# Storing the output of four batches by whole tiles, on one queue, in an attention and token-mixing kernel

## The chip, the cores and the metric

The kernel runs on one core of a Trainium2 chip. A core has five engines that run side by side, each through its own list of instructions: TensorE (PE: matrix multiplies, weight loads shown as PEld), VectorE (DVE), ScalarE (ACT), GpSimd (POOL) and SyncE (SP, which here issues only DMAs). Sixteen DMA engines move data between the device memory (DRAM) and the core's on-chip memory (SBUF, 128 partitions); a DMA is issued by an instruction on SyncE, ScalarE or GpSimd, and the three have queues of their own. In the profile GpSimd's queue is q0, SyncE's q1 and ScalarE's q10. The metric is the device time of one execution in microseconds (us); lower is better.

## The reference

For each of 8 batches, with 8 heads, 576 tokens and head size 64, a small set of 32 learned tokens attends to the tokens, and the tokens then attend to the 32 results. The heads are put side by side, and a token-mixing layer follows.

```python
p_packed = sm_attn(p, k, v)                 # 32 tokens per head
out = sm_attn(q, p_packed, p_packed)        # (8, 8, 576, 64)
x = out.transpose(0, 2, 1, 3).reshape(8, 576, 512)
W_tok = 0.125 * einsum('bsd,btd->bst', x @ w_q, x @ w_k)
mixed = einsum('bst,btd->bsd', W_tok, x)
return relu(mixed) @ w_out                  # (8, 576, 512), float32
```

The output has 8 x 576 x 512 float32 values, 9.44 MB.

## The kernel before, in words

The kernel has no loops over its work. The text ORDER (lines 12 to 56) is a schedule written out by hand: each word is a step with its batch, a part number, the engine that does it (A is ScalarE, V VectorE, P GpSimd; a step without a letter is TensorE's, or for a store SyncE's) and the PSUM banks. The launch loop at the end of the kernel (lines 597 to 619) reads the words one after another and calls the functions of those names. The order of the words is the order of the instructions on each engine and on each DMA queue; waits between engines follow from which tiles they share.

A batch goes through these steps. Its k, v and q come by LD steps on GpSimd's queue, which change float32 into bf16 on the way (lines 153 to 181). KT and QV transpose k and q on VectorE (lines 254 and 295 on). S1, X1, TE and PV are the first attention, QK the weights, S2, X2, RS, RR, AM the second attention (AM, line 404, is often on GpSimd), AT its transposes, WKQ, GM, Y and MX the token mixing, RL the relu, OT (line 526) the last matrix multiply, and OE and OEF (lines 544 and 547) the eviction of its result from PSUM into an output tile. All batches overlap: in the last 30 us the work of batches 5 to 7 runs while the output of the earlier batches is stored.

An output tile `o` is [128 partitions, 4, 512] float32. There are six of them (NO = 6, line 8), used in turn: batches 6 and 7 write into the tiles of batches 0 and 1, so their evictions wait until the stores of those have landed. A batch has 64 groups of 9 rows of the output. Eight rows of a group lie in two partitions of the tile, four rows of 2 KB in each; the function `orows` (line 541) gives this view of the output, as [64, 2, 2048]. The ninth rows of two batches together lie in one tile `orem`, [128, 512].

The stores are these steps:

- ST.b.n (line 554) with n of 0 or 1 stores one half of the tile of batch b: two rows of 512 from each partition, 4 KB in one piece, 512 KB in all.
- ST.b.4 stores the ninth rows of batches b - 1 and b: 2 KB from each partition, 256 KB.
- STF (line 587) stores a quarter of a tile in pieces of 2 KB, 256 KB, and STH (line 582) half of a quarter, 128 KB. They are used for batches 6 and 7 alone.

On SyncE's queue a step HOLD.v7 (line 566) stands ahead of all stores. It issues a tiny copy (to the tile `touch`) out of the last v tile, and so makes SyncE wait until that tile has landed. The stores behind it in SyncE's list therefore come after the loads of k and v. On GpSimd's queue the stores ST.1.1, ST.0.1 and ST.3.0 stand behind the last loads, LD.q7 and LD.r7 (the two halves of q of batch 7), and ST.5.1 stands at the end of GpSimd's list. SyncE's stores stand in this order: ST.2.1, ST.3.4, ST.4.0, ST.2.0, ST.0.0, ST.3.1, ST.5.4, ST.1.0, ST.4.1, then the stores of batches 5 to 7 as their data come.

Of the kernel before, what the change touches and what calls it, by code (L numbers as in the profile page):

```python
# [38 lines left out]
X2.5.2@A KT.6.2@V S2.5.3=6,7 X2.5.3@A HA.5@P WKQ.4.0=0,1 WKQ.4.2 LD.q7 WKQ.4.1 WE.4.2@A OT.3.0=2,3  # L39
S1.6=4,5,6,7 X1.6.0@A GM.4=0 GE.4@V TE.6.0@V LD.r7 OT.3.1 X1.6.1@A TE.6.1@V Y.4=0,1 OE.3.0@A RS.5.4@V RR.5.4@V  # L40
PV.6.0=4,5 YE.4@A PV.6.1 MX.4.0=6,7 RC.6@V RL.4.0@A PP.6.0@V AM.5.3@P PP.6.1@V PT.6@V MX.4.1=2,3 AM.5.2@P
OT.3.2=0,1 OT.3.3 RL.4.1@A QK.6=4 QKE.6@A QV.6.2@V ST.2.1 S2.6.2=6,7 X2.6.2@A S2.6.3=2,3 ST.3.4 MR.4=4,5
X2.6.3@A OE.3.1@V RLR.4@V KT.7.2@V AT.5.2=6 AE.5.2@A AT.5.3=7 OT.4.0=0,1 OT.4.1 AE.5.3@A WKQ.5.0=4,5 WKQ.5.2
OE.4.0@A ST.1.1@P WKQ.5.1 RS.6.4@V WE.5.2@A RR.6.4@V ST.4.0 ST.0.1@P S1.7=2,3,6,7 X1.7.1@A AM.6.3@V ST.3.0@P
OT.4.2=0,1 GM.5=4 TE.7.1@V OT.4.3 AT.6.3=5 X1.7.0@A TE.7.0@V GE.5@A OE.4.1@A AM.6.2@P AT.6.2=4 ST.2.0 Y.5=6,7
YE.5@A ST.0.0 ST.3.1 PV.7.0=2,3 QV.7.1@V AE.6.3@V QV.7.0@V AE.6.2@A QD.6@P PV.7.1 RC.7@V PP.7.0@V PP.7.1@V
PT.7@V MR.5=0,1 RLR.5@A MX.5.1=6,7 RL.5.1@A MX.5.0=4,5 RL.5.0@V WKQ.6.0=0,1 WKQ.6.1 WKQ.6.2 WE.6.2@A OT.5.4=2
OEF.5.4@A S2.7.1=6,7 ST.5.4 ST.1.0 GM.6=3 GE.6@V X2.7.1@A RS.7.1@V RR.7.1@V S2.7.2=0,1 X2.7.2@A S2.7.0=4,5
QK.7=2 X2.7.0@A RS.7.0@V RR.7.0@V Y.6=6,7 YE.6@A OT.5.2=0,1 MX.6.1=4,5 QKE.7@A MX.6.0=6,7 AM.7.1@P RS.7.2@V
RR.7.2@V MR.6=2,3 OT.5.3 RLR.6@V RL.6.0@V RL.6.1@A OE.5.1@A ST.4.1 AM.7.0@P OT.5.0=2,3 AM.7.2@P AT.7.0=4  # L50
AE.7.0@A AT.7.1=5 AE.7.1@V AT.7.2=6 AE.7.2@V OT.6.2=0,1 OEF.6.2@A QD.7@P WKQ.7.0=4,5 WKQ.7.2 WKQ.7.1 WE.7.0@A
WE.7.1@A STF.6.2 OT.6.0=6,7 OT.6.1 GM.7=0 OE.6.0@V OT.5.1 OE.5.0@V ST.5.1@P GE.7@A Y.7=4,5 OT.6.3 OEF.6.3@V
ST.6.0 STF.6.3 YE.7@A ST.5.0 MR.7=6,7 RLR.7@A MX.7.0=4,5 RLF.7.0.1@A RLF.7.0.0@V MX.7.1=2,3 RLF.7.1.0@A
OT.7.4=0 OEF.7.4@A ST.7.4 RLF.7.1.1@V OT.7.1=6 OEF.7.1@V OT.7.0=7 STF.7.1 OT.7.2=1 OEF.7.0@A OH.7.0=0 STF.7.0
OEF.7.2@A STF.7.2 OEH.7.0@V STH.7.0 OH.7.1=5 OEH.7.1@A STH.7.1@A
"""


# [1 line left out]
def kernel(  # L60
# [27 lines left out]
    P = 128  # L88
# [47 lines left out]
    def halves(x):  # L136
        return slice(x * 64, (x + 1) * 64)
# [79 lines left out]
    T = {}  # L217
# [323 lines left out]
    def orows(b):  # L541
        return out[b].rearrange("(g r) n -> g r n", r=R)[:, 0:8].rearrange("g (y t) n -> g y (t n)", y=2)
# [11 lines left out]
    def ST(b, n, eng, bk):  # L554
        q = {"A": nc.scalar, "P": nc.gpsimd}.get(eng, nc.sync)
        if n == 4:
            dst = out.rearrange("b (g r) n -> (b g) r n", r=R)
            q.dma_start(dst[(b - 1) * GR:(b + 1) * GR, R - 1], T["orem", b // 2])
        elif b in TURN:
            q.dma_start(orows(b)[:, :, n * 2 * D:(n + 1) * 2 * D],  # L560
                        T["o", b][:, 2 * n:2 * n + 2].rearrange("a t n -> a (t n)"))
        else:
            q.dma_start(orows(b)[:, n], T["o", b][halves(n)].rearrange("a t n -> a (t n)"))
# [23 lines left out]
    def STF(b, t, eng, bk):  # L587
# [4 lines left out]
                 PT=PT, QK=QK, QKE=QKE, QD=QD, QV=QV, S2=S2, X2=X2, HA=HA, RS=RS, RR=RR, AM=AM,  # L592
                 AT=AT, AE=AE, WKQ=WKQ, WE=WE, GM=GM, GE=GE, Y=Y, YE=YE, MX=MX, MR=MR, RL=RL, RLF=RLF,
                 RLR=RLR, OT=OT, OE=OE, OEF=OEF, ST=ST, STF=STF,
                 OH=OH, OEH=OEH, STH=STH)

    with tc.manual_schedule():
        for item in ORDER.split():
# [9 lines left out]
            elif f[0] == "WARM":  # L608
                n = 128 * int(f[1])
# [38 lines left out]
```

## Time and profile before

| | us |
|---|---|
| median of three runs | 105.13 |
| the three runs | 104.55, 105.13, 105.68 |
| the profiled execution | 104.06 |
| its span, first to last instruction | 102.2 |
| PE busy | 92.8 (91%) |
| DVE busy | 73.5 (72%) |
| ACT busy | 65.1 (64%) |
| POOL busy | 53.3 (52%) |

| DMA issues of the output | count, KB each | median us to landing |
|---|---|---|
| halves on SyncE | 9, 512 | 8.6 |
| halves on GpSimd | 4, 512 | 9.4 |
| quarters on SyncE | 5, 256 | 2.6 |
| ninth rows on SyncE | 3, 256 | 7.7 |
| ninth rows on GpSimd | 1, 256 | 14.4 |

How to read it: the busy share of an engine is an average over the span. The page also cuts the span into 40 slices of 2.56 us, in which a digit gives the busy share in tenths, and a row gives the GB/s that the DMA engines moved, counted as bytes written. "Landing" is the time from the issue of a DMA until its last byte is in place and its semaphore has been raised. In rows of instructions in order of time, the first column is the start and the second the duration, in us; a number in brackets is the idle time of the engine before the row, with what ended it. In rows of stages, each engine's busy time stands with its count of instructions, and the last columns are the granted clock of TensorE, the share of the DMA engines that was busy (a little over 1 where packets overlap) and the GB/s.

### The profile page before, as it was taken

To read this page: it belongs to the slowest core of one execution; us is meant where nothing else is said; L and a number is where in the kernel's file an instruction comes from. 1 tells how busy PE (TensorE), PEld (TensorE's weight loads), DVE (VectorE), ACT (ScalarE), POOL (GpSimd) and SP (SyncE) were. 2 spreads that over 40 slices of the span, in tenths; PEclk is the share of its full clock that TensorE was granted. 3 is DMA by queue.
4 is the path that set the end of the run, shared out by engine and by line. 5 is a ranking of instruction groups with operands and counts; after the bars stand their busy time and mean duration, and the time that the engine had idled before them with its cause. 6 is when DMAs were issued, how large, how long until landed. Compare 5 with 4: busy or idle time off the path is not lost.

```text
span 102.2 us, 3594 instructions
## 1 busy us (share of the span) xinstructions
PE 92.8 (91%) x1536; PEld 54.6 (53%) x1536; DVE 73.5 (72%) x140; ACT 65.1 (64%) x111; POOL 53.3 (52%) x83
## 2 busy tenths in 40 slices
PE   5997999998599999999998899989999999999940
PEld 3895445555275633755636556643757564743420
DVE  4273396858978579888697979599999979349510
ACT  1320315198654767849977979887989897726440
POOL 5982877974039929724459483649715009300000
PEclk9999999999999999999999999999999999999999
DMA  1999999999999999999999999999999999997894
GB/s 25 257 233 208 213 211 215 204 213 208 207 208 209 212 208 212 214 208 208 213 208 208 214 211 206 214 210 211 249 249 391 410 418 408 417 389 281 330 368 153
DMA packets 13567, 25.13 MB, mean 246 GB/s; under 512 B 1072, under 2 KB 6448, under 8 KB 13552
## 3 DMA queue, kind: packets, MB, share of 16 engines
q0 software_dynamic: 9936, 17.04, 84.6%
q1 hardware_dynamic: 3056, 7.34, 18.7%
q10 hardware_dynamic: 560, 0.52, 1.9%
q8 instruction: 12, 0.20, 0.7%
q14 instruction: 3, 0.02, 0.1%
HBM read 30.15 MB, written 9.44 MB: 387 GB/s over the span
## 4 chain that ended last, share of the span: by engine, by line
PE 50%; DMA 21%; DVE 8%; POOL 7%; ACT 7%; issue 3%; SPq 1%; POOLq 0%; DVEq 0%; ACTq 0%
PE ps L539 26%; DMA q_sb<-in_q_dram 13%; DMA o<-in_moe_w_q_dram 8%; PE ps L372 4%; POOL a L404 4%; PE ps L314 3%; ACT e1T L292 3%; PE ps L418 3%; PE ps L445 3%; DVE rs L393 2%; PE ps L440 2%; PE ps L466 2%; PE ps L281 2%; ACT e L377 1%; DVE qT L236 1%
## 5 line engine op out<-in xcount | busy, mean ns | idle before, releaser
L539 PE MATMUL ps<-wout,relu 128*128 128x512 bf16 x124 | 30.6, 380 | 0.0
L404 POOL TENSOR_TENSOR a<-e,rr 128x256 bf16<-128x256 f32 (+2 forms) x18 | 19.5, 1098 | 16.9 <-DVE rr L398 6.4
L614 PE MATMUL ps<-o 128*128 128x128 f32 (+3 forms) x76 | 19.3, 398 | 1.2 <-DVE o L134 1.2
L539 PEld LDWEIGHTS <-relu 128*128 128x128 bf16 x124 | 10.7, 98 | 11.7 <-issue 1.1
L127 ACT ACTIVATE o<-ps 128x1024 f32<-128x1024 f32 (+2 forms) x13 | 11.4, 878 | 5.4 <-PE ps L539 5.2
L614 PEld LDWEIGHTS ps<-o 128*128 128x128 f32 x76 | 11.2, 206 | 5.3 <-issue 3.6
L502 ACT ACTIVATE relu<-ps 128x1024 bf16<-128x1024 f32 (+1 forms) x14 | 12.9, 967 | 1.1 <-PE ps L491 1.1
L292 ACT ACTIVATE e1T<-ps 128x576 bf16<-128x576 f32 x16 | 9.8, 655 | 5.3 <-PE ps L281 4.7
L377 ACT ACTIVATE e<-ps 128x256 f32<-128x256 f32 (+2 forms) x19 | 11.2, 622 | 2.8 <-PE ps L372 2.6
L393 DVE TENSOR_REDUCE rs<-e 128x16 f32<-128x512 f32 (+2 forms) x13 | 10.9, 841 | 2.3 <-ACT e L377 2.2
L236 DVE STREAM_TRANSPOSE kT<-k_sb 128x1152 uint32<-128x1152 uint32 (+1 forms) x9 | 11.0, 1226 | 2.0 <-DMA k_sb<-in_k_dram 2.0
L172 POOL DMA_DIRECT2D v_sb<-in_v_dram x16 | 10.0, 629 | 4.6 <-DMA v_sb<-in_v_dram 1.4
L236 DVE STREAM_TRANSPOSE qT<-q_sb 128x1152 uint32<-128x1152 uint32 (+1 forms) x10 | 11.0, 1112 | 0.4 <-DMA q_sb<-in_q_dram 0.2
L131 DVE COPY o<-ps 128x1024 f32<-128x1024 f32 (+2 forms) x7 | 6.6, 958 | 5.0 <-PE ps L539 2.7
L236 DVE STREAM_TRANSPOSE e<-e1T 128x288 uint32<-128x288 uint32 x16 | 7.4, 469 | 2.5 <-ACT e1T L292 2.0
L127 ACT ACTIVATE aT<-ps 128x128 bf16<-128x128 f32 (+2 forms) x11 | 5.0, 465 | 5.7 <-PE ps L418 3.3
L314 PE MATMUL ps<-v_sb,e 64*64 64x192 bf16 x288 | 7.7, 245 | 0.8 <-DVE e L236 0.5
L127 ACT ACTIVATE wkq<-ps 128x448 bf16<-128x448 f32 (+1 forms) x10 | 7.2, 729 | 1.8 <-PE ps L445 1.7
L314 PEld LDWEIGHTS <-e 64*64 64x64 bf16 x288 | 6.0, 107 | 2.7 <-DVE e L236 2.0
L372 PEld LDWEIGHTS <-qT 64*128 64x128 bf16 x320 | 5.4, 94 | 2.8 <-DVE qT L236 1.8
L372 PE MATMUL ps<-ppT,qT 64*128 64x64 bf16 x320 | 6.6, 190 | 0.3 <-DVE qT L236 0.2
L445 PE MATMUL ps<-aT,pqk 128*128 128x256 bf16 (+1 forms) x48 | 6.8, 246 | 0.0
(70 smaller groups left out, 131.7 us busy)
## 6 DMA issues: line engine op xcount, KB each, us to landing
v_sb<-in_v_dram POOLq DMA_DIRECT2D x16, 288.0 KB, 14.3
out_dram<-o SPq DMA_DIRECT2D x9, 512.0 KB, 8.6
k_sb<-in_k_dram POOLq DMA_DIRECT2D x7, 576.0 KB, 13.8
q_sb<-in_q_dram POOLq DMA_DIRECT2D x6, 576.0 KB, 13.5
out_dram<-o POOLq DMA_DIRECT2D x4, 512.0 KB, 9.4
out_dram<-o SPq DMA_DIRECT2D x5, 256.0 KB, 2.6
q_sb<-in_q_dram POOLq DMA_DIRECT2D x4, 288.0 KB, 10.5
out_dram<-orem SPq DMA_DIRECT2D x3, 256.0 KB, 7.7
```

Source lines behind the costliest of these rows:

```text
L127: nc.scalar.activation(o, i, COPY)
L172: nc.gpsimd.dma_start(v_bufs[b % NL][halves(i), 0:7:2], src)
L236: nc.vector.transpose(o, i)
L292: nc.scalar.activation(e1T[:, x], T["s1", b][x].rearrange("a c m -> a m c"), EXP, scale=scale)
L314: nc.tensor.matmul(T["pv", b][halves(cc), i], lhsT, rhs, start=n == 0, stop=n == R - 1, skip_group_check=True)
L372: nc.tensor.matmul(ps[:, y, t - t0, i], lhsT, rhs, start=e == 0, stop=e == 1)
L377: nc.scalar.activation(e2[:, t0:t1].rearrange("a t (i y n) -> a y (t i) n", i=2, y=2), T["s2", b, c].rearrange("a y t i n -> a y (t i) n") ...
L393: nc.vector.tensor_reduce(rs[:, t0 * H:t1 * H], src, axis=AX, op=ADD)
L404: e.tensor_tensor(a2[:, t0:t1].rearrange("a t i (u l) -> a (t i u) l", l=L), e2v(b, c), T["rr", b][:, t0 * H:t1 * H].to_broadcast((P, (t1 ...
L502: nc.scalar.activation(o, i, RELU)
L539: nc.tensor.matmul(ps, lhsT, wout[:, j, :], start=j == 0, stop=j == NJ - 1)
L614: nc.tensor.matmul(bank(int(bk), [w]), warm[:, 0:P], rhs, start=True, stop=True)
```

## The change

The function ST gets a fourth case: with n = 8 it stores the whole tile of a batch, [128, 2048], into `orows(b)`, 8 KB in one piece from each partition, 1 MB in all. The eight half stores of batches 0 to 3 (three on GpSimd's queue, five on SyncE's) go, and four whole ones on SyncE's queue take their place. ST.5.1, the second half of batch 5, moves from GpSimd's queue to SyncE's, at the same place in the text. SyncE's stores stand now in the order ST.3.4, ST.1.8, ST.0.8, ST.2.8, ST.3.8, ST.4.0, ST.5.4, ST.4.1, STF.6.2, ST.5.1, ST.6.0, STF.6.3, ST.5.0, and then those of batch 7 as before. GpSimd's queue keeps one store, ST.1.4. No other step changes its engine or its place among the steps of its engine.

The diff of ORDER, cut to the lines in which the stores stood and stand:

```diff
-OT.3.2=0,1 OT.3.3 RL.4.1@A QK.6=4 QKE.6@A QV.6.2@V ST.2.1 S2.6.2=6,7 X2.6.2@A S2.6.3=2,3 ST.3.4 MR.4=4,5
...
-OE.4.0@A ST.1.1@P WKQ.5.1 RS.6.4@V WE.5.2@A RR.6.4@V ST.4.0 ST.0.1@P S1.7=2,3,6,7 X1.7.1@A AM.6.3@V ST.3.0@P
-OT.4.2=0,1 GM.5=4 TE.7.1@V OT.4.3 AT.6.3=5 X1.7.0@A TE.7.0@V GE.5@A OE.4.1@A AM.6.2@P AT.6.2=4 ST.2.0 Y.5=6,7
-YE.5@A ST.0.0 ST.3.1 PV.7.0=2,3 QV.7.1@V AE.6.3@V QV.7.0@V AE.6.2@A QD.6@P PV.7.1 RC.7@V PP.7.0@V PP.7.1@V
...
-OEF.5.4@A S2.7.1=6,7 ST.5.4 ST.1.0 GM.6=3 GE.6@V X2.7.1@A RS.7.1@V RR.7.1@V S2.7.2=0,1 X2.7.2@A S2.7.0=4,5
...
-WE.7.1@A STF.6.2 OT.6.0=6,7 OT.6.1 GM.7=0 OE.6.0@V OT.5.1 OE.5.0@V ST.5.1@P GE.7@A Y.7=4,5 OT.6.3 OEF.6.3@V
+OT.3.2=0,1 OT.3.3 RL.4.1@A QK.6=4 QKE.6@A QV.6.2@V S2.6.2=6,7 X2.6.2@A S2.6.3=2,3 ST.3.4 ST.1.8 ST.0.8 ST.2.8
...
+WKQ.5.2 OE.4.0@A WKQ.5.1 RS.6.4@V WE.5.2@A RR.6.4@V ST.3.8 ST.4.0 S1.7=2,3,6,7 X1.7.1@A AM.6.3@V OT.4.2=0,1
...
+OE.6.0@V OT.5.1 OE.5.0@V ST.5.1 GE.7@A Y.7=4,5 OT.6.3 OEF.6.3@V ST.6.0 STF.6.3 YE.7@A ST.5.0 MR.7=6,7 RLR.7@A
```

The diff of ST:

```diff
         if n == 4:
             dst = out.rearrange("b (g r) n -> (b g) r n", r=R)
             q.dma_start(dst[(b - 1) * GR:(b + 1) * GR, R - 1], T["orem", b // 2])
+        elif n == 8:
+            q.dma_start(orows(b), T["o", b].rearrange("a t n -> a (t n)"))
         elif b in TURN:
             q.dma_start(orows(b)[:, :, n * 2 * D:(n + 1) * 2 * D],
```

More of the change, by code (lines that the diff above doesn't have):

```diff
@@ L41 @@
 PV.6.0=4,5 YE.4@A PV.6.1 MX.4.0=6,7 RC.6@V RL.4.0@A PP.6.0@V AM.5.3@P PP.6.1@V PT.6@V MX.4.1=2,3 AM.5.2@P
-OT.3.2=0,1 OT.3.3 RL.4.1@A QK.6=4 QKE.6@A QV.6.2@V ST.2.1 S2.6.2=6,7 X2.6.2@A S2.6.3=2,3 ST.3.4 MR.4=4,5
-X2.6.3@A OE.3.1@V RLR.4@V KT.7.2@V AT.5.2=6 AE.5.2@A AT.5.3=7 OT.4.0=0,1 OT.4.1 AE.5.3@A WKQ.5.0=4,5 WKQ.5.2
-OE.4.0@A ST.1.1@P WKQ.5.1 RS.6.4@V WE.5.2@A RR.6.4@V ST.4.0 ST.0.1@P S1.7=2,3,6,7 X1.7.1@A AM.6.3@V ST.3.0@P
-OT.4.2=0,1 GM.5=4 TE.7.1@V OT.4.3 AT.6.3=5 X1.7.0@A TE.7.0@V GE.5@A OE.4.1@A AM.6.2@P AT.6.2=4 ST.2.0 Y.5=6,7
@@ L46 @@
-YE.5@A ST.0.0 ST.3.1 PV.7.0=2,3 QV.7.1@V AE.6.3@V QV.7.0@V AE.6.2@A QD.6@P PV.7.1 RC.7@V PP.7.0@V PP.7.1@V
-PT.7@V MR.5=0,1 RLR.5@A MX.5.1=6,7 RL.5.1@A MX.5.0=4,5 RL.5.0@V WKQ.6.0=0,1 WKQ.6.1 WKQ.6.2 WE.6.2@A OT.5.4=2
-OEF.5.4@A S2.7.1=6,7 ST.5.4 ST.1.0 GM.6=3 GE.6@V X2.7.1@A RS.7.1@V RR.7.1@V S2.7.2=0,1 X2.7.2@A S2.7.0=4,5
-QK.7=2 X2.7.0@A RS.7.0@V RR.7.0@V Y.6=6,7 YE.6@A OT.5.2=0,1 MX.6.1=4,5 QKE.7@A MX.6.0=6,7 AM.7.1@P RS.7.2@V
-RR.7.2@V MR.6=2,3 OT.5.3 RLR.6@V RL.6.0@V RL.6.1@A OE.5.1@A ST.4.1 AM.7.0@P OT.5.0=2,3 AM.7.2@P AT.7.0=4
@@ L51 @@
-AE.7.0@A AT.7.1=5 AE.7.1@V AT.7.2=6 AE.7.2@V OT.6.2=0,1 OEF.6.2@A QD.7@P WKQ.7.0=4,5 WKQ.7.2 WKQ.7.1 WE.7.0@A
-WE.7.1@A STF.6.2 OT.6.0=6,7 OT.6.1 GM.7=0 OE.6.0@V OT.5.1 OE.5.0@V ST.5.1@P GE.7@A Y.7=4,5 OT.6.3 OEF.6.3@V
-ST.6.0 STF.6.3 YE.7@A ST.5.0 MR.7=6,7 RLR.7@A MX.7.0=4,5 RLF.7.0.1@A RLF.7.0.0@V MX.7.1=2,3 RLF.7.1.0@A
-OT.7.4=0 OEF.7.4@A ST.7.4 RLF.7.1.1@V OT.7.1=6 OEF.7.1@V OT.7.0=7 STF.7.1 OT.7.2=1 OEF.7.0@A OH.7.0=0 STF.7.0
-OEF.7.2@A STF.7.2 OEH.7.0@V STH.7.0 OH.7.1=5 OEH.7.1@A STH.7.1@A
+OT.3.2=0,1 OT.3.3 RL.4.1@A QK.6=4 QKE.6@A QV.6.2@V S2.6.2=6,7 X2.6.2@A S2.6.3=2,3 ST.3.4 ST.1.8 ST.0.8 ST.2.8
@@ new lines @@
+MR.4=4,5 X2.6.3@A OE.3.1@V RLR.4@V KT.7.2@V AT.5.2=6 AE.5.2@A AT.5.3=7 OT.4.0=0,1 OT.4.1 AE.5.3@A WKQ.5.0=4,5
+WKQ.5.2 OE.4.0@A WKQ.5.1 RS.6.4@V WE.5.2@A RR.6.4@V ST.3.8 ST.4.0 S1.7=2,3,6,7 X1.7.1@A AM.6.3@V OT.4.2=0,1
+GM.5=4 TE.7.1@V OT.4.3 AT.6.3=5 X1.7.0@A TE.7.0@V GE.5@A OE.4.1@A AM.6.2@P AT.6.2=4 Y.5=6,7 YE.5@A PV.7.0=2,3
+QV.7.1@V AE.6.3@V QV.7.0@V AE.6.2@A QD.6@P PV.7.1 RC.7@V PP.7.0@V PP.7.1@V PT.7@V MR.5=0,1 RLR.5@A MX.5.1=6,7
+RL.5.1@A MX.5.0=4,5 RL.5.0@V WKQ.6.0=0,1 WKQ.6.1 WKQ.6.2 WE.6.2@A OT.5.4=2 OEF.5.4@A S2.7.1=6,7 ST.5.4 GM.6=3
@@ new lines @@
+GE.6@V X2.7.1@A RS.7.1@V RR.7.1@V S2.7.2=0,1 X2.7.2@A S2.7.0=4,5 QK.7=2 X2.7.0@A RS.7.0@V RR.7.0@V Y.6=6,7
+YE.6@A OT.5.2=0,1 MX.6.1=4,5 QKE.7@A MX.6.0=6,7 AM.7.1@P RS.7.2@V RR.7.2@V MR.6=2,3 OT.5.3 RLR.6@V RL.6.0@V
+RL.6.1@A OE.5.1@A ST.4.1 AM.7.0@P OT.5.0=2,3 AM.7.2@P AT.7.0=4 AE.7.0@A AT.7.1=5 AE.7.1@V AT.7.2=6 AE.7.2@V
+OT.6.2=0,1 OEF.6.2@A QD.7@P WKQ.7.0=4,5 WKQ.7.2 WKQ.7.1 WE.7.0@A WE.7.1@A STF.6.2 OT.6.0=6,7 OT.6.1 GM.7=0
+OE.6.0@V OT.5.1 OE.5.0@V ST.5.1 GE.7@A Y.7=4,5 OT.6.3 OEF.6.3@V ST.6.0 STF.6.3 YE.7@A ST.5.0 MR.7=6,7 RLR.7@A
@@ L56 @@
+MX.7.0=4,5 RLF.7.0.1@A RLF.7.0.0@V MX.7.1=2,3 RLF.7.1.0@A OT.7.4=0 OEF.7.4@A ST.7.4 RLF.7.1.1@V OT.7.1=6
+OEF.7.1@V OT.7.0=7 STF.7.1 OT.7.2=1 OEF.7.0@A OH.7.0=0 STF.7.0 OEF.7.2@A STF.7.2 OEH.7.0@V STH.7.0 OH.7.1=5
+OEH.7.1@A STH.7.1@A
 """
```

## The prediction

> **What bounds the kernel now.** I read the page's slices first, then the chain that ended last, then SyncE's and GpSimd's instructions in order of time, then the DMA packets stage by stage.
>
> ```profile
> span 102.2 us, 3594 instructions
> PE   5997999998599999999998899989999999999940
> DMA  1999999999999999999999999999999999997894
> GB/s 25 257 233 208 213 211 215 204 213 208 207 208 209 212 208 212 214 208 208 213 208 208 214 211 206 214 210 211 249 249 391 410 418 408 417 389 281 330 368 153
> PE 50%; DMA 21%; DVE 8%; POOL 7%; ACT 7%; issue 3%; SPq 1%; POOLq 0%; DVEq 0%; ACTq 0%
> ```
>
> TensorE and the 16 DMA engines are both full almost to the end. Loads run to slice 29 (about 76 us) at about 210 GB/s of written bytes; from slice 30 the output goes out at about 410 GB/s. TensorE makes up half of the chain. So the change, which touches only stores, can move the end in three ways: through the last stores, through a buffer that comes free late, or through the last loads.
>
> ```profile
> 75.52 0.62 SPq L571 DMA_DIRECT2D touch<-v_sb  x1
> 76.18 0.63 SPq L560 DMA_DIRECT2D out_dram<-o  x1
> 76.85 0.60 SPq L558 DMA_DIRECT2D out_dram<-orem  x1
> 77.49 3.31 SPq L560 DMA_DIRECT2D out_dram<-o  x4
> 89.05 0.54 SPq L589 DMA_DIRECT2D out_dram<-o  x1
> 92.19 0.54 SPq L560 DMA_DIRECT2D out_dram<-o  x1
> 94.02 0.54 SPq L589 DMA_DIRECT2D out_dram<-o  x1
> 94.61 0.59 SPq L560 DMA_DIRECT2D out_dram<-o  x1
> 96.57 2.11 SPq L589 DMA_DIRECT2D out_dram<-o  x3
> 98.77 0.56 SPq L585 DMA_DIRECT2D out_dram<-o  x1
> ```
>
> SyncE is held by the touch (75.52) until the last v tile has landed; only then does it issue stores. The rows from 89.05 on are stores of batches 5 to 7, each waiting for its data.
>
> ```profile
> 66.59 1.09 POOL L178 DMA_DIRECT2D q_sb<-in_q_dram  x2
> 71.66 1.89 POOL L560 DMA_DIRECT2D out_dram<-o  x3
> 76.18 1.58 POOL L404 TENSOR_TENSOR a<-e,rr 128x256 bf16<-128x256 f32 x1 [2.64 <-DVE rr L398]
> 87.51 0.66 POOL L560 DMA_DIRECT2D out_dram<-o  x1 [0.30 <-ACT o L127]
> ```
>
> On GpSimd's queue three half stores (71.66) stand behind the last two q loads (66.59).
>
> ```profile
> 76.00:77.00 1.00, 1.00 (x12) 0.53 (x12) 0.96 (x2) 1.00 (x2) 0.82 (x1) 1.00 1.08 326
> 77.00:78.00 1.00, 1.00 (x14) 0.53 (x11) 0.94 (x3) 0.90 (x3) 0.99 (x2) 1.00 1.02 382
> 91.00:96.00 5.00, 4.95 (x37) 1.99 (x34) 4.34 (x6) 2.62 (x6) 0.00 (x0) 1.00 0.74 291
> 96.00:101.00 5.00, 2.35 (x15) 1.27 (x13) 0.96 (x2) 1.58 (x3) 0.00 (x0) 1.00 0.97 359
> ```
>
> The last two columns of these stages are the DMA engines' share and GB/s. They are full from 76 us on, have 26% of 5 us, so 1.3 us, idle between 91 and 96, and are full again in the tail.
>
> **The change part by part.** The execution shown took 104.06 us, of which 102.2 are its span, 1.86 lying around it. The runs have a median of 105.13 (104.55 to 105.68), 1.07 above it. I sum against 104.06 and carry the difference over.
>
> *GpSimd's four stores go.* Issuing them takes 1.89 + 0.66 = 2.55 us of GpSimd. After the first three it waits 2.64 us for VectorE's rr anyway, and the fourth is its last work. Gain on the path: 0. If that cover were gone, the gain would be up to 1.89 us at the 76.18 row.
>
> *SyncE's instructions.* Eight half stores of batches 0 to 3 (three on GpSimd, five on SyncE) become four whole ones on SyncE, and the half of batch 5 moves from GpSimd to SyncE, behind the store of 89.05. Issues that pass on SyncE cost about 0.6 us each. After the touch it now issues the remainder, four whole stores and half of batch 4: six in a row, as many as before, all before the next data at 82 us. Batch 5's half is issued at about 89.6 instead of 87.5, and SyncE is free again before 92.19. In the built program a store on SyncE also waits for the landing of the eighth before it; with whole stores the tightest of these is the store of 94.61, behind batch 3's landing at about 89. Cost 0.
>
> *Buffer reuse.* Batches 6 and 7 write into the tiles of batches 0 and 1, which now go out second and third on SyncE, by about 83 us (start at 77.4 below, 0.7 + 2.5 + 2.5 us). The first eviction into them starts at
>
> ```profile
> 88.43 0.60 ACT L127 ACTIVATE o<-ps 128x512 f32<-128x512 f32 x1 [0.55 <-PE ps L539]
> ```
>
> and waited for TensorE. With 5 us to spare the cost is 0.
>
> *The hole behind the loads.* This is the part with a price. Which queue had the engines while loads ended:
>
> ```profile
> DMA packets 106, 0.33 MB, mean 326 GB/s; under 512 B 8, under 2 KB 8, under 8 KB 106
> q0 software_dynamic: 106, 0.33, 107.9%
> DMA packets 112, 0.38 MB, mean 382 GB/s; under 512 B 14, under 2 KB 14, under 8 KB 112
> q0 software_dynamic: 112, 0.38, 101.8%
> touch<-v_sb SPq DMA_DIRECT2D x1, 0.1 KB, 5.7
> ```
>
> The first pair is 76 to 77 us, the second 77 to 78. All packets are GpSimd's (q0). Beside 8 and 14 small ones there are 98 in each; as q packets have 2304 bytes (a row of 18 x 64 values in bf16) and halves 4096, 0.326 MB makes 42 loads and 56 stores, 0.382 MB makes 11 and 87. So GpSimd's stores filled the engines as the loads thinned out. They are now on SyncE, whose first store is issued at 76.18. Its data starts later: the shortest landing of the page's issues, 2.1 us for 128 KB (quoted below), leaves about 1.8 us beside its 0.34 us of transfer, for lead and completion together. I take 1.2 of it as lead, so a start at 77.4; bounds are 76.2 and 78.0. Work displaced until 77.4: 56 x 4096 B / 414 GB/s = 0.55 us, and 0.4 of 87 x 4096 / 414 = 0.34: 0.9 us. Bounds: 0.1 (a start at 76.2) and 1.4.
>
> *Rows of 8 KB.* No store here has them. Rows near:
>
> ```profile
> DMA packets 758, 2.49 MB, mean 414 GB/s; under 512 B 87, under 2 KB 87, under 8 KB 757
> DMA packets 318, 0.58 MB, mean 389 GB/s; under 512 B 33, under 2 KB 33, under 8 KB 318
> q8 instruction: 12, 0.20, 0.7%
> ```
>
> 84 to 90 us, 97.5 to 99 us, and the page's instruction fetches. The second is nearly pure 2 KB: 285 packets in 16 x 1.5 us, 84 ns each. The first has 671 of 2 and 4 KB with 2.49 MB, so 546 of 4 KB and some 125 of 2 KB; 96 us of engine time less 10.5 leaves 157 ns for 4 KB. The second 2 KB cost 73 ns, so 8 KB would take 84 + 3 x 73 = 303 ns against 314 for two of 4 KB. Each engine has 32 of them (4 stores x 128 rows / 16): 0.35 us gained. From the other side, the 16 KB fetches took 0.7% x 16 x 102.2 / 12 = 954 ns, 477 for 8 KB: 32 x (477 - 314) = 5.2 us lost. They are another kind of transfer and the stores' own rows are nearer, so I take -0.35.
>
> The Trainium skill, "DMA: Bandwidth & Descriptors", section "Anatomy of one DMA — SWDGE (gpsimd) path", fits a DMA's time as 2.0 us plus bytes over 436 GB/s, which favours fewer, larger ones. By it four DMAs fewer would save some 8 us, an estimate from that page, if they ran one after another; the 414 GB/s with 512 KB stores shows that here they overlap.
>
> *Sum.* 0.9 - 0.35 = +0.55 us of DMA backlog by 91 us (from 0.1 - 0.35 = -0.25 to 1.4 without the gain; the fetches' rate would make it 6.1), against 1.3 us of idle DMA between 91 and 96. It is covered. Without that cover it would delay the tail one to one. The tail itself keeps its stores:
>
> ```profile
> 98.39 0.38 ACT L127 ACTIVATE o<-ps 128x256 f32<-128x256 f32 x1 [0.28 <-PE ps L576]
> 98.81 0.64 ACTq L585 DMA_DIRECT2D out_dram<-o  x1
> out_dram<-o SPq DMA_DIRECT2D x1, 128.0 KB, 2.1
> out_dram<-o ACTq DMA_DIRECT2D x1, 128.0 KB, 2.5
> ```
>
> The last eviction ends at 98.8, its store lands at 101.3, and 0.9 us of closing follow. End change 0: 104.1 for the profiled execution, 105.1 on the runs' scale.
>
> **The rivals.** *Slow rows (slower).* If an 8 KB packet takes t ns, the backlog is 0.9 + 0.032 x (t - 314) us and passes the cover at t = 327; the end is over 1% (1.05 us) late from t = 360. Half way to the fetches' rate, t = 390, it is 0.9 + 2.4 - 1.3 = 2.0 us: 107.1. For it: no store shows such a packet, and a hole of 0.9 has eaten most of the cover. Against: time per byte falls from 2 to 4 KB.
>
> *Stores overtake the last q loads.* GpSimd's stores stood behind them in one queue; SyncE's do not.
>
> ```profile
> DMA to landing us min/median/max: 10.9/11.3/11.7
> 79.40 0.76 DVE L236 STREAM_TRANSPOSE qT<-q_sb 128x576 uint32<-128x576 uint32 x1
> 80.89 0.31 DVE L236 STREAM_TRANSPOSE ppT<-pp 128x128 uint32<-128x128 uint32 x1
> 81.94 0.41 PE L372 MATMUL ps<-ppT,qT 64*128 64x64 bf16 x16
> ```
>
> The second q load, issued at 67.1, landed by 78.8; its transpose starts at 79.40, and the ppT behind it is done 0.7 us before TensorE's use: 1.3 us of room. An engine with six loads left, alternating with 8 KB rows, would lose 6 x 303 = 1.8 us, 0.5 over the room: 105.6. Against: the remainder's 2 KB rows come first now (6 x 84 = 0.5 us, inside the room), and while q0 had work no SyncE packet moved, not even the touch, which took 5.7 us.
>
> The skill's same page, section "Queues, rings and completion order", says that each engine takes turns between queues that have work, packet by packet; by that rule this rival's 105.6 would hold. The two microseconds without a SyncE packet after the touch's issue speak against it in this stage.
>
> *The tail drains sooner.* If the backlog ended early and the last stores met no queue, the last landing would take 2.1 us, as the row of SyncE's last store, instead of 2.5: 104.7. For it: DMA share 0.97 in the tail. Against: that is the tail's own stores, which stay.
>
> *The rows are split to 4 KB anyway.* Then 0.35 us of gain is missing, 0.9 stays under the cover: 105.1.
>
> **How the numbers follow.** No change 0.58, split rows 0.07 (same time), overtaken loads 0.12, slow rows 0.15, sooner tail 0.08. About 1% is what a measurement can tell from no change. Slower by over 1%: slow rows 0.15, a third of the overtaken loads 0.04, and 0.02 of scatter of the median (the three runs lie within 0.5% of it): 0.21. Faster: a third of the sooner tail and scatter, 0.08. Same: 0.71. The range takes in the sooner tail (104.7, less 0.4 of scatter) and the overtaken loads, and reaches into slow rows: 104.3 to 106.5.
>
> **What would show it.** In the profile after: no q0 store packets after 76 us and a dip in GB/s near 76.5 to 77.5 (the hole); packets of 8 KB and GB/s above 414 between 80 and 88 (the rows); VectorE's q transposes still at about 78.2 and 79.4 (loads not overtaken); DMA share above 0.74 between 91 and 96 (backlog into the cover); ScalarE's last eviction still near 98.4 and the last landing near 101.3. A q transpose after 80.7, or DMA share 1.0 through 91 to 96 with the last landing later, would prove me wrong.

## The result, and the profile after

The changed kernel is slightly slower: 104.88 us against 104.58 us (medians of 21 runs each). The ratio is 1.0034 with a 95% interval of 1.0019 to 1.0048, which is 0.36 us; the two medians alone are 0.30 us apart. I had forecast no change, and the sum had the end move by 0. That 104.88 us lies near the forecast 105.1 is in part luck: 105.1 stood on a median of three runs (105.13), and 21 runs of the kernel before have a median of 104.58. The profiled execution took 104.99 us. It is 0.9 us over that of the kernel before (104.06), so the pair of profiles shows more than the medians do: 0.22 us of it is a shift of the whole computation, which is there before the first store of SyncE, and the rest (0.71 us) lies behind the last eviction. The sizes that follow from this pair are those of two executions; the 0.36 us is what 21 runs give.

The slices of the page, then five stages with the DMA engines' share and GB/s in the last two columns:

```profile
span 103.2 us, 3588 instructions
GB/s 10 241 230 209 213 209 213 207 207 214 205 210 209 211 207 214 211 210 207 212 211 206 213 213 203 215 213 207 253 177 352 426 419 410 387 405 344 395 371 75
```

```profile
76.00:77.00 1.00, 1.00 (x36) 0.41 (x5) 0.97 (x2) 1.00 (x3) 0.60 (x1) 1.00 0.76 143
77.00:78.00 1.00, 1.00 (x15) 0.64 (x14) 0.93 (x3) 1.00 (x3) 1.00 (x2) 1.00 0.73 208
78.00:80.00 2.00, 2.00 (x60) 1.62 (x58) 2.00 (x4) 1.60 (x5) 0.22 (x1) 1.00 0.99 385
91.00:96.00 5.00, 4.95 (x40) 2.11 (x39) 4.26 (x5) 2.62 (x6) 0.00 (x0) 1.00 0.94 368
96.00:101.00 5.00, 2.58 (x16) 1.37 (x14) 1.12 (x2) 1.58 (x3) 0.00 (x0) 1.00 1.01 381
```

The dip of slice 29 (177 GB/s, counted from 0) is the hole: between 76 and 78 us the engines moved 0.35 MB, where before they had moved 0.71 MB. Between 91 and 96 the share rose from 0.74 to 0.94: the backlog ran into the idle time that I had counted as cover, and nearly filled it on the mean of the engines.

SyncE's first instructions after the hold, ScalarE's last eviction and store, and the landing times of the last stores (last column, us from issue to landing):

```profile
75.83 0.62 SPq L573 DMA_DIRECT2D touch<-v_sb  x1
76.50 0.58 SPq L558 DMA_DIRECT2D out_dram<-orem  x1
77.12 4.44 SPq L560 DMA_DIRECT2D out_dram<-o  x4
```

```profile
98.61 0.39 ACT L127 ACTIVATE o<-ps 128x256 f32<-128x256 f32 x1 [0.28 <-PE ps L578]
99.03 0.64 ACTq L587 DMA_DIRECT2D out_dram<-o  x1
```

```profile
out_dram<-o SPq DMA_DIRECT2D x1, 256.0 KB, 3.1
out_dram<-o SPq DMA_DIRECT2D x1, 128.0 KB, 2.9
out_dram<-o ACTq DMA_DIRECT2D x1, 128.0 KB, 3.2
```

The last store landed 3.2 us after its issue instead of 2.5, and SyncE's last 2.9 instead of 2.1. The evictions were not held up: the last one starts 0.22 us later, as everything from 66 us on does. So the time was lost between the issue of the last stores and their landing. The open questions were whether the hole did it, whether the 8 KB rows or the moved half of batch 5 had a part, and whether the kernel before really had cover.

### The profile page after: what moved, and what is told of

Same layout as the page of the kernel before. It is cut to its first block, busy times and chain, and to the rows that moved or that the text cites. A ratio compares the mean times of both kernels' runs of the same rounds, so it can differ in the third digit from the quotient of the medians.

```text
span 103.2 us, 3588 instructions
## 1 busy us (share of the span) xinstructions
PE 93.3 (90%) x1536; PEld 55.2 (54%) x1536; DVE 73.9 (72%) x140; ACT 65.1 (63%) x111; POOL 50.7 (49%) x79
## 4 chain that ended last, share of the span: by engine, by line
PE 62%; DVE 9%; ACT 9%; DMA 7%; POOL 4%; issue 3%; POOLq 0%; DVEq 0%; ACTq 0%
PE ps L539 25%; PE ps L616 8%; DMA k_sb<-in_k_dram 7%; PE ps L372 5%; ACT e1T L292 4%; PE ps L314 4%; POOL a L404 4%; PE ps L418 3%; PE ps L445 3%; PE ps L281 2%; DVE rs L393 2%; PE ps L440 2%; PE ps L335 2%; PE ps L466 2%; DVE kT L236 2%
## 5 line engine op out<-in xcount | busy, mean ns | idle before, releaser
L616 PE MATMUL ps<-o 128*128 128x128 f32 (+3 forms) x76 | 19.9, 408 | 1.2 <-DVE o L134 1.2
L616 PEld LDWEIGHTS ps<-o 128*128 128x128 f32 x76 | 11.7, 216 | 5.3 <-issue 3.6
```

The costliest lines, as they stand in the source:

```text
L616: nc.tensor.matmul(bank(int(bk), [w]), warm[:, 0:P], rhs, start=True, stop=True)
```

## The experiments

Each run is compared with the kernel before on its own chip. Theory A: the hole behind the loads makes a backlog that reaches the last stores. Theory B: the 8 KB rows are slow. Theory C: the half of batch 5, now in SyncE's one queue, holds up the stores behind it.

**Halves on SyncE's queue** (e1): the four whole stores cut in two again, at the same places.

```diff
-ST.1.8 ST.0.8 ST.2.8
+ST.1.0 ST.1.1 ST.0.0 ST.0.1 ST.2.0 ST.2.1
...
-ST.3.8
+ST.3.0 ST.3.1
```

> The changed kernel with its four whole stores cut in two again: halves with rows of 4 KB, all on SyncE's queue at the same places. Theory A (the engines run dry between the last loads and SyncE's first store, 76 to 77.5 us, and the backlog reaches the last stores): the hole stays, share about 0.75 between 76 and 78, time 1.002 to 1.005 of before as with the change. Theory B (the 8 KB rows are what is slow: their packets and all others show 2 to 3% over the shortest duration from 77 us on): the time returns to before, 0.998 to 1.001, with packets at their shortest again.

Measured: 1.0081 (1.005 to 1.0112). The hole is there, and the kernel is slower than with whole stores. Stages of this run:

```profile
76.00:77.00 1.00, 0.95 (x35) 0.50 (x36) 0.93 (x3) 1.00 (x2) 0.32 (x1) 1.00 0.84 157
77.00:78.00 1.00, 1.00 (x14) 0.58 (x13) 1.00 (x2) 1.00 (x3) 1.00 (x1) 1.00 0.98 314
91.00:96.00 5.00, 4.95 (x40) 2.16 (x39) 4.25 (x5) 2.58 (x6) 0.00 (x0) 1.00 0.90 352
```

Theory B falls: without the 8 KB rows the time did not return. Theory A had the hole right and this size wrong (1.002 to 1.005). Of the 0.49 us between this run and the changed kernel, 0.24 us lie behind the last landing and not in the stores (see e9). The hole of this execution is the smaller one (0.47 MB between 76 and 78 us, where the changed kernel moved 0.35): its hold was released 0.56 us earlier.

**Two whole stores on GpSimd's queue** (e2): ST.1.8 and ST.0.8 go behind the last q loads, where halves had stood.

```diff
-ST.1.8 ST.0.8 ST.2.8
+ST.2.8
...
-OE.4.0@A WKQ.5.1
+OE.4.0@A ST.1.8@P WKQ.5.1
...
-X1.7.1@A AM.6.3@V
+X1.7.1@A ST.0.8@P AM.6.3@V
```

> The changed kernel with two of the four whole stores (batches 1 and 0) on GpSimd's queue where the halves of before stood, behind the last q loads. Theory A: no hole (share 1.0 or more between 76 and 78), tail landings back from 3.2 to about 2.5 us, time 0.997 to 1.001 of before. Theory B: rows of 8 KB remain, time stays at 1.002 to 1.005.

Measured: 1.0018 (0.9996 to 1.0039), not told from no change. The hole is filled (shares 1.17 and 1.08 between 76 and 78), the share between 91 and 96 is 0.78, and the last stores land after 2.1 and 2.5 us, as in the kernel before. The profile answers to theory A; the time lies just above what it expected, and its interval takes in both. The stretch from the last landing to the end of the span is 0.12 us longer here than in the kernel before (1.10 against 0.98), which is most of the 0.19 us by which the time is longer.

**An earlier hold** (e3): SyncE waits for the first half of the last v tile only; everything else is the changed kernel.

```diff
-        src = src[64:96, 4, 0:2] if x[0] == "v" else ...
+        src = src[0:32, 4, 0:2] if x[0] == "v" else ...
```

> The changed kernel, but SyncE waits for the first half of the last v tile only, which lands some 1.5 us before the second. Theory A: SyncE's stores start at about 74.5 instead of 76.5, the hole is closed, time 0.997 to 1.001 of before, unless the stores now slow the last q loads, whose transposes would then start after 78.4 and 79.6. Theory B: 1.002 to 1.005 as with the change.

Measured: 0.9997 (0.9983 to 1.0012). SyncE's touch, the stages, and which queue had the engines between 76 and 78 us (packets, MB, share):

```profile
74.28 0.62 SPq L573 DMA_DIRECT2D touch<-v_sb  x1
```

```profile
76.00:77.00 1.00, 0.95 (x35) 0.50 (x36) 0.93 (x3) 1.00 (x2) 0.31 (x1) 1.00 1.10 268
77.00:78.00 1.00, 1.00 (x14) 0.58 (x13) 1.00 (x2) 1.00 (x3) 1.00 (x1) 1.00 1.09 385
91.00:96.00 5.00, 4.95 (x40) 2.14 (x39) 4.26 (x5) 2.58 (x6) 0.00 (x0) 1.00 0.75 295
```

```profile
q1 hardware_dynamic: 185, 0.45, 58.1%
q0 software_dynamic: 97, 0.18, 48.6%
```

With the touch 1.5 us earlier the hole is gone, the idle time between 91 and 96 is back (0.75), the last stores land after 2.1 and 2.5 us, and the loss is gone. Here SyncE's packets (q1) moved while q loads (q0) were still moving; the two q transposes started at 78.68 and 79.91, in a run whose last eviction too is 0.5 us later than before (98.91). Relative to the computation they were not late.

**The half of batch 5 back on GpSimd's queue** (e4), and **only this half moved in the kernel before** (e11):

```diff
-OE.5.0@V ST.5.1 GE.7@A
+OE.5.0@V ST.5.1@P GE.7@A
```

The second is the reverse edit, made in the kernel before.

> The changed kernel with the second half of batch 5 back on GpSimd's queue (issued at about 87.5 instead of 89.9). Theory C (this store, ahead of batch 6's in SyncE's one queue, delays the tail): time back to 0.998 to 1.001 of before. Theories A and B: the backlog is the same on either queue, 1.002 to 1.005.

> The kernel before with only the second half of batch 5 moved from GpSimd's queue to SyncE's. If this move has a part in the change's loss (theory C), 1.001 to 1.003 of before and tail landings above 2.5 us. If it matters only on top of a backlog (theory A), 0.998 to 1.001 with tail landings of 2.1 and 2.5 us.

Measured: 1.0023 (1.0009 to 1.0037) and 0.9993 (0.9972 to 1.0015). In the kernel before, the move costs nothing (tail landings 2.1 and 2.5). With the hole, undoing it leaves most of the loss (last landings 2.5 and 2.8, between those of the changed kernel and those of the kernel before); whether it gives back the 0.1 points between 1.0034 and 1.0023 the intervals do not tell. The hole of that execution was smaller too: 0.27 MB displaced between 76 and 78 us, against 0.36. Theory C falls as the main cause.

**A later hold** (e5): a second touch makes SyncE wait for the last q load too.

```diff
-S2.6.3=2,3 ST.3.4 ST.1.8
+S2.6.3=2,3 HOLD.r7 ST.3.4 ST.1.8
...
-        z = 2 * int(x[0] == "h")
+        z = 2 * int(x[0] in "hr")
```

> The changed kernel with a second touch, which makes SyncE wait for the last q load as well (about 2.5 us later than the v tile), so that the hole is about 2.5 us longer. Theory A (the hole reaches the last stores, as the cover behind it is used up): the end moves by most of it, time 1.015 to 1.028 of before, tail landings 2 us longer than with the change. Rival (the hole is covered and the change's loss has another cause): time stays within 1.002 to 1.008.

Measured: 1.037 (1.0345 to 1.0395), above what I expected, because the second touch came later than I had reckoned. SyncE's rows, the stages and the landings:

```profile
79.23 0.53 SPq L573 DMA_DIRECT2D touch<-q_sb  x1
79.81 0.58 SPq L558 DMA_DIRECT2D out_dram<-orem  x1
```

```profile
79.00:80.00 1.00, 1.00 (x42) 0.95 (x43) 1.00 (x3) 0.99 (x2) 0.00 (x0) 1.00 0.00 0
91.00:96.00 5.00, 4.95 (x40) 2.12 (x39) 4.18 (x5) 2.21 (x6) 0.00 (x0) 1.00 1.01 393
```

```profile
out_dram<-o SPq DMA_DIRECT2D x3, 256.0 KB, 5.1
out_dram<-o ACTq DMA_DIRECT2D x1, 128.0 KB, 4.3
```

The first store is issued at 79.81 instead of 76.50, 3.3 us later, and the time is (1.037 - 1.0034) x 104.6 = 3.5 us longer. There is no idle time left between 91 and 96. Beyond the hole of the changed kernel, this one run has a longer hole go into the time about one to one. The landings grew by less than the 2 us that I expected (SyncE's last store takes 3.5 us instead of 2.9, ScalarE's 4.3 instead of 3.2), because the delay shows earlier: in the backlog SyncE issues its last store at 102.09 instead of 99.00.

**One tile less to store**, in the changed kernel (e6) and in the kernel before (e7):

```diff
-ST.0.8 ST.2.8
+ST.0.8
```

In the kernel before, ST.2.1 and ST.2.0 are taken out.

> The changed kernel without the store of batch 2's tile (1 MB, 2.5 us of the DMA engines), which leaves batch 2's output unwritten. Theory A: the hole stays but the backlog behind it is gone before 91 us; tail landings back to about 2.1 and 2.5 us, time 0.996 to 1.000 of before. Rival (the last stores are slow for another reason, such as the order on SyncE's queue): tail landings stay near 3 us, time above 1.002.

> The kernel before without the two half stores of batch 2, which leaves batch 2's output unwritten. If the kernel before has cover for its backlog, as predicted, nothing moves: 0.997 to 1.001 of before, tail landings 2.1 and 2.5 us. If its backlog too reaches the last stores, the time falls below 0.995.

Measured: 1.0012 (0.9994 to 1.003) and 1.0004 (0.999 to 1.0018). The stage from 91 to 96 and the last landings, of the changed kernel with a tile less, then the stage of the kernel before with a tile less:

```profile
91.00:96.00 5.00, 4.95 (x40) 2.14 (x39) 4.26 (x5) 2.62 (x6) 0.00 (x0) 1.00 0.69 267
```

```profile
out_dram<-o SPq DMA_DIRECT2D x1, 128.0 KB, 2.2
out_dram<-o ACTq DMA_DIRECT2D x1, 128.0 KB, 2.5
```

```profile
91.00:96.00 5.00, 4.95 (x41) 2.06 (x38) 4.25 (x5) 2.33 (x6) 0.00 (x0) 1.00 0.44 170
```

In the kernel before, taking away 1 MB empties the stage (0.74 to 0.44), leaves the last landings at 2.1 and 2.5 us and gains nothing: its backlog did not reach the end, as predicted. In the changed kernel 1 MB less brings the last landings from 2.9 and 3.2 us back to 2.2 and 2.5, with the hole, SyncE's order and the other 8 KB rows as they were. The hole of this run is as large as that of the changed kernel (143 and 199 GB/s in the two microseconds). The time (1.0012) is a little over the expectation, and its interval takes in no change.

**Earlier hold and halves** (e9): both edits of e1 and e3.

> The changed kernel with the earlier hold and with its four whole stores cut into halves of 4 KB rows, all on SyncE's queue. If the loss is the hole alone and rows of 4 KB cost only what they did in the kernel before (413 GB/s between 80 and 87 us), the time is that of before, 0.998 to 1.001, with tail landings of 2.1 and 2.5 us. If rows of 4 KB on SyncE's queue are slow without a hole too (401 GB/s, as in the run with halves and the hole), part of its loss remains: 1.002 to 1.005.

Measured: 1.0027 (1.0013 to 1.0041). There is no hole, the rows move at 411 GB/s, and the last stores land after 2.2 and 2.5 us, as the first theory said; the time is that of the second. With the changed kernel, e1 and e3 this makes a table of two factors, ratios to the kernel before:

| | rows of 4 KB, eight stores | rows of 8 KB, four stores |
|---|---|---|
| hold of the change | 1.0081 | 1.0034 |
| earlier hold | 1.0027 | 0.9997 |

The hole costs 0.54 and 0.37 points (0.56 and 0.39 us), the whole rows gain 0.47 and 0.30 (0.49 and 0.31 us). By the intervals of the four ratios each of these differences is known to 0.2 to 0.35 points only.

What the whole stores gain is not all a matter of rows. ScalarE's last store is issued and lands at nearly the same times in e9 and e3:

```profile
99.31 0.64 ACTq L587 DMA_DIRECT2D out_dram<-o  x1
99.33 0.64 ACTq L587 DMA_DIRECT2D out_dram<-o  x1
```

Both land 2.5 us later, at 101.8, and yet the span of e9 ends at 103.00 and that of e3 at 102.77. At the end SyncE waits for the semaphores of the stores one after another, some 0.06 us each, and the semaphore of the last store does not have the same place in that order in every kernel. In e3 one more wait follows the last landing, in e9 five. From the last landing to the end of the span it is 1.22 us with halves on SyncE's queue (e1 and e9) and 0.98 in the kernel before, with the change, in e3 and in e8. So 0.24 us of the whole stores' gain are this end, and 0.25 and 0.07 us are left.

**A quarter and a half exchanged, with the earlier hold** (e8): a try at a faster version.

```diff
-ST.6.0 STF.6.3 YE.7@A ST.5.0
+ST.6.0 ST.5.0 STF.6.3 YE.7@A
```

> The changed kernel with the earlier hold (first half of the last v tile), and with the second half of batch 5 (ST.5.0) ahead of the quarter STF.6.3 instead of behind it, so that its 512 KB go out while the engines idle between 93 and 95 us. If the tail is a queue of its own from 95.5 us on, it is shorter by up to 0.5 us: 0.994 to 0.999 of before, share in 91 to 96 up from 0.75 to 0.85. If the last landing is only the last store's own latency, it stays at 0.998 to 1.002.

Measured: 0.9992 (0.9977 to 1.0006), no different from before. The share between 91 and 96 rose to 0.87 and that between 96 and 101 fell to 0.91, as meant, but the last store still landed 2.5 us after its issue. This order did not get below it. Its first packet moved 1.59 us after its issue, as in the kernel before (1.59), with the change (1.60) and in e3 (1.59); SyncE's packets filled the engines until then (a share of 1.07 between 100.4 and 100.6). Whether it would land sooner on idle engines was not tried. No version here beats the kernel before by more than the scatter.

## Why the prediction was wrong

**GpSimd's and SyncE's instructions: right.** GpSimd waits 4.46 us instead of 2.64 for VectorE and nothing else changes; SyncE is ready for every later store in time. The move of batch 5's half costs nothing by itself (0.9993).

**Buffer reuse and the last loads: right.** The first eviction into a reused tile started at 88.65, 0.22 later like all else, and waited for TensorE. The q transposes started at 78.39 and 79.62, again some 0.2 later. The stores did not overtake the loads to their harm. What I took as the reason, that no SyncE packet moves while GpSimd's queue has work, does not hold: with the earlier hold both queues had about half of the engines between 76 and 78, and in the kernel before SyncE's first packets moved at 79.4 while GpSimd's queue still had 84.5% of the engines' time in that microsecond. The trace with the earlier hold agrees with the rule of the Trainium skill that I had weighed ("DMA: Bandwidth & Descriptors", section "Queues, rings and completion order"): the engines take turns between queues. Why SyncE's touch and first store moved nothing for over 3 us in the kernel before, no run here shows. The loads had room all the same, so this part came out right for a wrong reason.

**The hole: right in size.** Displaced between 76 and 78 us: (326 + 382) - (143 + 208) = 357 GB/s for 1 us, 0.36 MB, 0.86 us at 414 GB/s. The sum had 0.9. In two more executions with the same stores up to 78 us it was 0.64 (e4) and 0.88 us (e6). The lead of 1.2 us that I took was near too: from the issue of SyncE's first store to its first packet it is 1.06 us with the change, 1.09 in e3 and 1.07 in e5, where the engines were idle.

**The 8 KB rows: right in sign, and near in size on the DMA engines.** The stage from 80 to 87 us, in the kernel before, with the change, and with halves on SyncE's queue:

```profile
DMA packets 881, 2.89 MB, mean 413 GB/s; under 512 B 98, under 2 KB 98, under 8 KB 880
```

```profile
DMA packets 405, 2.94 MB, mean 420 GB/s; under 512 B 47, under 2 KB 47, under 8 KB 47
```

```profile
DMA packets 763, 2.81 MB, mean 401 GB/s; under 512 B 81, under 2 KB 81, under 8 KB 762
```

Rows of 8 KB move at 420 against 413 GB/s, 1.7% where I had 3.5%. The packet records say it directly: from 77 us on an 8 KB row takes 309 ns at the shortest and 312 in the median with the change, and two 4 KB rows take 2 x 159 = 318 in the kernel before. For 32 rows that is 0.2 to 0.3 us, where the sum had 0.35. That the table of e9 shows 0.31 and 0.49 us, around that figure, is in part luck, since 0.24 us of each lie behind the last landing. The rate of the instruction fetches, my upper bound (477 ns), is not that of the stores. The fit of the Trainium skill ("DMA: Bandwidth & Descriptors", section "Anatomy of one DMA — SWDGE (gpsimd) path"), 2 us per DMA on GpSimd's path, would have four DMAs fewer gain some 8 us, an estimate from that page, if they ran one after another. Here they overlap, and the runs show at most 0.5 us.

**The sum's last step failed: "It is covered."** The rows of the stages show by how much. Compared with before, the changed kernel had moved 0.36 MB less by 78 us, 0.04 MB less again by 80, 0.05 MB more between 80 and 87, and 4 us x (416 - 392) = 0.10 MB less between 87 and 91, the last two numbers being the rates of that stage in the two traces. That is a backlog of 0.44 MB at 91 us, 1.07 us at 414 GB/s, where the sum had 0.55. (Loads and hold ended about 0.3 us later in this execution, which is part of it.) Against 1.3 us of idle time even this looked covered, and yet the last landings grew by 0.7 us, and the last one came at 102.2 where the prediction had 101.3.

The 1.3 us was a mean over 16 engines, and a store has landed only when the last of its engines is done. The trace tells the engines apart at the landing: it keeps 16 rises of a semaphore for each of these stores, as many as there are engines, and I read each rise as one engine done. Of the store ST.6.0, issued at 92.19 before and 92.42 with the change, and of the last store they come at these times (us):

| | first | 8th | 14th | 15th | last |
|---|---|---|---|---|---|
| ST.6.0, kernel before | 95.00 | 95.08 | 95.28 | 95.87 | 96.00 |
| ST.6.0, with the change | 95.26 | 95.36 | 96.28 | 96.91 | 97.14 |
| last store, kernel before | 101.11 | 101.17 | 101.24 | 101.25 | 101.27 |
| last store, with the change | 101.34 | 101.42 | 101.55 | 102.07 | 102.19 |

At the last store 14 of the 16 engines are back within 0.1 us of the time before plus the shift of 0.22 us: for them the delay was covered. Two engines are 0.5 and 0.6 us behind these, and the store waits for them. At ST.6.0 the engine that came last was 1.14 us later than before, 0.92 beyond the shift, which is as much as the hole (0.86). For that engine next to nothing of the 1.3 us was cover: already in the kernel before it came 0.72 us after the 14th at ST.6.0, and the idle time belonged mostly to the others. It made up some 0.2 us by the end. The DMA row of the profile shows the same, here from 98.5 to 103 us in slices of 0.11 us, for the kernel before, the change and e3; where it falls to 1, about two engines of 16 are at work:

```profile
DMA  9998996799899999999950000000000000000000
DMA  9999999997999999999999711111100000000000
DMA  9899889999949999999999999300000000000000
```

From the 13th rise to the last it is 0.70 us for the last store with the change, 0.53 in e1, 0.39 in e4 and 1.34 in e5, the four runs with a hole and all their stores. In the kernel before and in the seven other runs it is 0.04 to 0.06. So it is shown that the cover was there in the kernel before (a tile less gains nothing), that the hole used it up on the engines that end last (a longer hole goes into the time, a tile less brings the landings back), and that without the hole the loss is gone (0.9997).

**What stays open.** Why one or two engines run behind is not shown. There is a trail: a fetch of instructions (16 KB on one engine) takes 0.88 to 0.97 us in these two traces. One begins at 71.44 in the kernel before; of the landing at 71.49 the last rise comes 0.06 us after the 15th, of the next, at 73.99, 1.17 us. With the change the last two fetches begin at 86.53 and 92.67, in the kernel before at 84.63 and 92.28. That these put the two late engines behind is argued, as the packet records do not name the engine. The last landing of the profiled execution was late by 0.7 us, about twice the 0.36 us of the medians; e4, with a smaller hole, shows 0.3 us, so the delay seems to differ from one execution to the next. The halves' 0.27% with the earlier hold is 0.28 us, of which the end behind the last landing makes up 0.24.

## What to carry to other kernels

Before you move transfers from one queue to another, look at what they fill: here the stores behind the last loads kept the DMA engines busy until the other queue's first store had its data on the way, and that was worth 0.4 to 0.6 us, more than the 0.2 to 0.3 us that the longer rows save. A mean idle share over a stage is not cover for a delay: a store waits for the last of its engines, so ask how far that one is behind the others, and look at the spread of the landings, not at the mean. Where a hold keeps stores off the loads, release it ahead of the last load by the time that the first store needs from its issue to its first packet (1.1 us here). And before a few tenths of a us are put down to transfers, look at what the program does after the last landing.

## What the runs showed of the hardware that was not expected

In one pair of traces 4 KB rows moved more slowly after a hole: 401 GB/s between 80 and 87 us with halves on SyncE's queue (e1), against 411 with the same stores and the earlier hold (e9):

```profile
DMA packets 785, 2.88 MB, mean 411 GB/s; under 512 B 86, under 2 KB 86, under 8 KB 784
```

The rate of 8 KB rows differs less (420 with the change, 423 with the earlier hold). The cause was not tried.

The Trainium skill says ("DMA: Bandwidth & Descriptors", section "Issuing engines are not separate DMA queues") that DMAs of all issuing engines run on the same 16 DMA engines, and that spreading them over several saves only the time of issuing. In the steady stage the runs agree: between 80 and 87 us whole stores move at 420 GB/s from SyncE's queue alone (the change) and at 420 from two queues (e2, GpSimd's with 29.3% of the engines' time):

```profile
DMA packets 525, 2.94 MB, mean 420 GB/s; under 512 B 68, under 2 KB 68, under 8 KB 203
q1 hardware_dynamic: 397, 2.06, 71.4%
q0 software_dynamic: 127, 0.86, 29.3%
```

At the change from loads to stores the queue did matter: there it decided when the first store could start, and with it 0.4 us of time.
